# Channel blocks opened during the first batch's tail, V placed by GpSimd, pair 12 prepared a pair sooner, weights issued later

## Chip, cores and metric

One core of a Trainium2 chip. The metric is the device time of the kernel in microseconds (us), launch to end; the span in a profile is some 1.8 us shorter. Runs of one kernel scatter by up to 4 us here, mostly for a reason that the experiments show, so medians are given with the runs' granted TensorE clocks (1.0 is full rate, and the mean over a run is given). All runs with a recorded state are in the fast state. In the lines of the profile PE is TensorE, DVE VectorE, ACT ScalarE, POOL GpSimd and SPq SyncE, which issues DMAs; L with a number is a line of the kernel.

## The reference

Cosine attention for 8 batches, 12 heads, 448 positions, 64 channels a head, then a low-rank mixer and a channel network on the 768 channels:

```python
q_n = q / (norm(q) + 1e-06); k_n = k / (norm(k) + 1e-06)
attn = softmax(q_n @ k_n.T / tau)
x = attn @ v                                  # laid out as [batch, 448, 768]
h = x.transpose(0, 2, 1) @ U @ V              # rank 32
u = x + h.transpose(0, 2, 1)
out = u + relu(u @ w_ch1) @ w_ch2             # 768 -> 3072 -> 768
```

## The kernel before

The 48 pairs of heads (8 batches of 6) are numbered 0 to 47 and handled in groups, mostly of two pairs. A group's q, k and v are loaded by SyncE's queue, squared (ScalarE or GpSimd), reduced (VectorE), rooted (ScalarE), inverted, and q and k scaled. The scaled blocks are transposed by TensorE, from pair 12 on by the DMA. The first batch runs by a hand-written list of words; from pair 6 on, each pair's attention is interleaved with "fill" steps, the channel network of the batch before: 24 blocks of six matmuls with w1 (m1), then 24 steps of six matmuls with w2 (m2). The first batch's 48 steps are spread over pairs 6 to 12.

```python
# the tail of the first batch's list: w7 is seven filler matmuls, A, XT, H the mixer's steps,
# Ac and U its evictions, w1_i the issue of a quarter of w1 (GpSimd's DMA queue)
... V50 Ac4.v XT4 X50 V51 sq4k H4 X51
w7 U4.a A5 red4q Ac5.a XT5 H5 U5.a red4k w1_2 root4 w1_3 inv4 sc6q.v sc6k.v
# (cut)
load_w2(0, 0, 12); load_w2(0, 12, 24)
preps[4].values()
fill.extend(steps_m1(0) + steps_m2(0))
f(5)                       # five blocks ahead of pair 6's transposes
T(NP)
# (cut) preparation of pair 12's group: when its squares, reductions, root, scalings run
elif m == 2 * NP:
    at = [(m - 2, 0), (m - 2, 0), (m - 2, 6), (m - 2, 4), (m - 2, 3), (m - 2, 5)]
    when = [(m - 1, 0)] * 4
# (cut) loads: of pair m's group, by SyncE; the program order is the queue's order
put(m - 6, 4, lambda gi=gi: load(gi, "q", nc.sync))
put(m - 5, 5, lambda gi=gi: load(gi, "k", nc.sync))
put(m - 4, 3, lambda gi=gi: load(gi, "v", nc.sync))
```

Of the kernel before, what the change touches and what calls it, by code (L numbers as in the profile page):

```python
# [22 lines left out]
def kernel(  # L23
# [17 lines left out]
    nc = tc.nc  # L41
# [106 lines left out]
    def place_v(copy, rows):  # L148
        lo = V_raw[rows, 0:256].rearrange("r (p c) -> r c p", c=4)
        hi = V_raw[rows, 256:448].rearrange("r (p c) -> r c p", c=3)  # L150
        body = V_sb[rows, 0:384].rearrange("r (c p) -> r c p", p=128)
        copy(out=body[:, :, 0:64], in_=lo[:, 0:3, :])
        copy(out=body[:, :, 64:128], in_=hi)
        copy(out=V_sb[rows, 384:448], in_=lo[:, 3, :])

    def place_mixer():
        nc.scalar.copy(out=U_sb[:, :, 0:R], in_=U_raw)
        place_v(nc.scalar.copy, slice(0, R))

    def load_copies():  # L160

# [10 lines left out]
    def load_w2(half, n0, n1):  # L172
        cols = slice(half * HC, (half + 1) * HC)
        nc.gpsimd.dma_start(
            out=w2_sb[:, n0:n1, cols],
            in_=moe_w_ch2[n0 * 128:n1 * 128, cols].rearrange("(n p) d -> p n d", p=128))
# [407 lines left out]
    def f(n):  # L584
        for _ in range(n):
            fill.pop(0)()
# [18 lines left out]
    def T(n):  # L605
        step_T(*pairs[n])
# [10 lines left out]
    def Hs(n):  # L617
# [3 lines left out]



    ORDER = """
        sq0k.a red0k sq0q.a red0q root0 inv0 sc0q.v sc0k.v l3q l3k l2v w62 T0 sq1q.a sq1k.p w11
        Te0 red1q S00 sq2k.p S01 ex00 red1k w8 root1 S02 w26 sq2q.a inv1 red2k sc1k.p ex01 sc1q.p
        red2q ex02 S03 w6 ex03 val0 l3v T1 root2 val1 l4q l4k l4v V00 Te1 place inv2 S10 V01
        sc2q.v S11 ex10 w9 sc2k.v ex11 X01 sc3k.p S12 T2 X00 ex12 S13 sc3q.p Te2 A0 w3 sq3q.a
        Ac0.v S20 T3 sq3k.a w19 red3q ex13 red3k ex20 S21 V10 ex21 w1_0 V11 X10 S22 Te3 root3 val2
        l5q l5k l5v S23 ex22 inv3 XT0 H0 X11 sc4q.p ex23 S30 U0.v ex30 V20 sc4k.v S31 A1 ex31 S32  # L630
        X20 sc5q.p T4 Ac1.v ex32 Te4 V21 sc5k.p S33 X21 XT1 ex33 S40 val3 H1 ex40 A2 U1.v S41 V30
        Ac2.v ex41 S42 X30 T5 ex42 V31 Te5 S43 X31 ex43 S50 XT2 ex50 A3 S51 Ac3.v H2 V40 ex51 U2.v
        S52 X40 V41 w1_1 ex52 S53 X41 XT3 sq4q ex53 H3 A4 U3.a V50 Ac4.v XT4 X50 V51 sq4k H4 X51
        w7 U4.a A5 red4q Ac5.a XT5 H5 U5.a red4k w1_2 root4 w1_3 inv4 sc6q.v sc6k.v
    """
    bank1 = psum.tile([128, 512], FP, name="mp", tag="ps_m", bufs=2)
    spare = psum.tile([128, 512], FP, name="mp", tag="ps_m", bufs=2)
    copies = {"a": nc.scalar.copy, "v": nc.vector.tensor_copy}
    QK = {"q": 0, "k": 1}

    def word(w):
        w, _, eng = w.partition(".")
        if w.startswith("w1_"):
            i = int(w[3:])
            load_w1(768 * i, 768 * (i + 1))
        elif w[0] == "w":
            for _ in range(int(w[1:])):
                nc.tensor.matmul(out=spare[:, 0:128], lhsT=ident, rhs=ident, start=True, stop=True)
        elif w[0] == "l":
            load(int(w[1]), w[2], nc.sync)  # L650
        elif w == "place":
            place_mixer()
        elif w.startswith("sq"):
            preps[int(w[2])].square(QK[w[3]], eng == "a")
        elif w.startswith("red"):
            preps[int(w[3])].reduce(QK[w[4]])
        elif w.startswith("root"):
            preps[int(w[4])].root()
        elif w.startswith("inv"):
            preps[int(w[3])].invert()  # L660
        elif w.startswith("val"):
            preps[int(w[3])].values()
        elif w.startswith("sc"):
            gi, j = group_of[pairs[int(w[2])]]
            preps[gi].scale(QK[w[3]], j, {"v": V_, "p": P_}[eng])
        elif w.startswith("Te"):
            evict_T(*pairs[int(w[2])])
        elif w.startswith("ex"):
            exp_S(*pairs[int(w[2])], int(w[3]))
        elif w.startswith("XT"):  # L670
            pe_XT(*pairs[int(w[2])])
        elif w.startswith("Ac"):
            evict_A(*pairs[int(w[2])], copies[eng])
        else:
            at = pairs[int(w[1])]
            if w[0] == "T":
                pe_T(*at)
            elif w[0] == "S":
                pe_S(*at, int(w[2]))
            elif w[0] == "V":  # L680
                half = int(w[2])
                pe_V(*at, half, bank1 if half else
                     psum.tile([128, 512], FP, name="av", tag="ps_av", bufs=1))
            elif w[0] == "X":
                divide_V(*at, int(w[2]))
            elif w[0] == "A":
                pe_A(*at)
            elif w[0] == "H":
                pe_H(*at)
            else:  # L690
                assert w[0] == "U", w
                evict_H(*at, copies[eng])

    for w in ORDER.split():
        word(w)
    load_w2(0, 0, 12)
    load_w2(0, 12, 24)
    preps[4].values()
    fill.extend(steps_m1(0) + steps_m2(0))
    f(5)  # L700
    T(NP)
    preps[4].scale(0, 1, V_)
    preps[4].scale(1, 1, V_)
# [8 lines left out]
    for gi in range(5, len(groups)):  # L712
        m, g = first_pair[gi], preps[gi]
        scales = [(1, 0, P_), (1, 1, P_), (0, 0, V_), (0, 1, V_)]
        if m == NP + 2:
            at = [(NP, 0), (NP, 1), (NP + 1, 6), (NP, 5), (NP + 1, 0), (NP + 1, 1)]
            when = [(NP + 1, 2), (NP + 1, 5), (NP + 1, 2), (NP + 1, 5)]
            scales = [(1, 0, V_), (1, 1, V_), (0, 0, V_), (0, 1, V_)]
        elif m == NP + 4:
            at = [(NP + 2, 0), (NP + 2, 1), (NP + 2, 6), (NP + 2, 3), (NP + 2, 5), (NP + 2, 6)]  # L720
            when = [(NP + 3, 0), (NP + 3, 0), (NP + 3, 1), (NP + 3, 3)]
        elif m == 2 * NP:
            at = [(m - 2, 0), (m - 2, 0), (m - 2, 6), (m - 2, 4), (m - 2, 3), (m - 2, 5)]
            when = [(m - 1, 0)] * 4
            scales = [(1, 0, P_), (0, 0, P_), (1, 1, P_), (0, 1, P_)]
        else:
            d = 1 if m == 2 * NP + 2 else 0
            at = [(m - 3, 0), (m - 3, 0), (m - 3, 5)] + [(m - 2, i + d) for i in (1, 0, 2)]
            when = [(m - 2, i + d) for i in (3, 3, 4, 5)]

        put(*at[1], lambda g=g: g.square(1))
        put(*at[0], lambda g=g: g.square(0))
        put(*at[2], lambda g=g: g.values())
        put(*at[4], lambda g=g: g.reduce(1))
        put(*at[3], lambda g=g: g.reduce(0))
        put(*at[5], lambda g=g: g.root())
        put(*when[0], lambda g=g: g.invert())
        for x, w in zip(scales, when):
            put(*w, lambda g=g, x=x: g.scale(*x))
        if gi > 5 and m - 6 <= NP:  # L740
            put(*((NP, 3), (NP + 3, 0))[gi - 6], lambda gi=gi: load_all(gi))
        elif gi > 5:
            put(m - 6, 4, lambda gi=gi: load(gi, "q", nc.sync))
            put(m - 5, 5, lambda gi=gi: load(gi, "k", nc.sync))
            put(m - 4, 3, lambda gi=gi: load(gi, "v", nc.sync))
        if by_dma(m):
            put(m - 1, -1 if m > 2 * NP else 2, lambda m=m: T(m))
            put(m - 1, 0 if m > 2 * NP else 4, lambda m=m: T(m + 1))

    put(NP, 2, lambda: (load_w2(1, 0, 12), load_w2(1, 12, 24)))  # L750
    put(NP + 3, 0, load_copies)
    put(NP + 5, 6, place_copies)

# [16 lines left out]
    for n in range(NP, NPAIR + 1):  # L770
# [7 lines left out]
        if not late:  # L778
            if n % 2 == 0:

                order = [
                    (1, lambda: Sc(n, 0, 1)),
                    (0, done and (lambda: V(n - 1, 0))),
                    (1, None if by_dma(n + 1) else (lambda: T(n + 1))),
                    (0, lambda: Sc(n, 3)),
                    (1, done and (lambda: V(n - 1, 1))),
                    (0, done and (lambda: A(n - 1))),
                    (1, lambda: (Sc(n, 2), Sc(n + 1, 0))),
                    (1, done and (lambda: Hs(n - 1))),
                ]  # L790
            else:
                order = [
                    (1, lambda: Sc(n, 1, 2)),
                    (1, lambda: V(n - 1, 0)),
                    (0, lambda: Sc(n, 3)),
                    (1, lambda: V(n - 1, 1)),
                    (1, not by_dma(n + 1) and (lambda: T(n + 1))),
                    (1, lambda: A(n - 1)),
                    (0, lambda: Hs(n - 1)),
                ]  # L800
            last = p == 0 and done
            nf = len(fill) if last else 5
            spread(n, order, nf)
            if last:
                f(len(fill))
                fill.extend(steps_m1(b - 1) + steps_m2(b - 1))
            continue
# [80 lines left out]
```

## Time and profile before

| | kernel before |
|---|---|
| median of the 4 runs beside the changed kernel | 588.94 us (587.92 to 589.08) |
| TensorE busy | 571.9 of 585.8 us |
| wait of PE at pair 12 (for the DMA transposes) | 2.40 us, then 3.4 us at half clock |
| transposes of pair 12: issued, landed | 93.91 us, 100.23 us |
| w2's last part landed | 97.6 us |

Landings are read from the DMA records of the trace. The lines that carry the argument stand in the prediction. What to look for in them: PE is full from 105 us to the end, so everything that the change can win lies before, and there the DMA share is about 1.

### The profile page before, as it was taken

To read this page: it belongs to the slowest core of one execution; us is meant where nothing else is said; L and a number is where in the kernel's file an instruction comes from. 1 tells how busy PE (TensorE), PEld (TensorE's weight loads), DVE (VectorE), ACT (ScalarE), POOL (GpSimd) and SP (SyncE) were. 2 spreads that over 40 slices of the span, in tenths; PEclk is the share of its full clock that TensorE was granted. 3 is DMA by queue.
4 is the path that set the end of the run, shared out by engine and by line. 5 is a ranking of instruction groups with operands and counts; after the bars stand their busy time and mean duration, and the time that the engine had idled before them with its cause. 6 is when DMAs were issued, how large, how long until landed. Compare 5 with 4: busy or idle time off the path is not lost.

```text
span 585.8 us, 12308 instructions
## 1 busy us (share of the span) xinstructions
PE 571.9 (98%) x5087; PEld 329.4 (56%) x5087; DVE 260.9 (45%) x503; ACT 260.8 (45%) x449; POOL 187.7 (32%) x162
## 2 busy tenths in 40 slices
PE   7999998999999999999999999999999999999997
PEld 6664564655555555554565555655556555655564
DVE  7875762525345355544454265543455342220011
ACT  5965544265334555346423465345442474214200
POOL 8674356504145055234053142252250410000000
PEclk9999999999999999999999999999999999999999
DMA  6999999455375684684464754873645631222012
GB/s 166 203 235 234 236 239 230 115 118 120 79 160 129 123 144 113 133 172 94 107 148 120 163 110 99 159 159 84 139 119 122 135 64 25 59 62 44 8 47 55
DMA packets 138584, 74.25 MB, mean 127 GB/s; under 512 B 85568, under 2 KB 138352, under 8 KB 138528
## 3 DMA queue, kind: packets, MB, share of 16 engines
q1 hardware_dynamic: 128256, 62.77, 48.2%
q0 software_dynamic: 9728, 10.18, 10.2%
q8 instruction: 40, 0.66, 0.5%
q10 hardware_dynamic: 544, 0.51, 0.3%
q14 instruction: 16, 0.13, 0.1%
HBM read 52.19 MB, written 11.01 MB: 108 GB/s over the span
## 4 chain that ended last, share of the span: by engine, by line
PE 88%; DMA 5%; DVE 2%; issue 1%; ACT 1%; SPq 1%; POOL 1%; POOLq 0%; DVEq 0%
PE mp L538 36%; PE mp L511 35%; PE sc L329 5%; PE av L381 3%; PE up L381 2%; DMA qst<-in_q_dram 2%; DVE qk L269 1%; DMA vst<-in_v_dram 1%; DMA qkT<-qk 1%; PE av L374 1%; PE av L341 1%; PE tp L298 1%; PE up L374 1%; PE up L467 1%; ACT E L354 1%
## 5 line engine op out<-in xcount | busy, mean ns | idle before, releaser
L538 PE MATMUL mp<-w_sb,relu 128*128 128x384 bf16 x1344 | 234.8, 328 | 0.0
L538 PEld LDWEIGHTS <-relu 128*128 128x128 bf16 x1344 | 125.9, 98 | 90.5 <-issue 14.5
L511 PEld LDWEIGHTS <-w_sb 128*128 128x128 bf16 x1152 | 107.4, 98 | 101.4 <-issue 10.1
L515 ACT ACTIVATE relu<-mp 128x448 bf16<-128x448 f32 x164 | 89.1, 543 | 131.2 <-PE mp L511 131.2
L354 ACT ACTIVATE E<-sc 128x896 bf16<-128x896 f32 x144 | 125.0, 923 | 23.6 <-PE sc L329 22.7
L269 POOL TENSOR_TENSOR qk<-kst,inv 128x512 bf16<-128x512 f32 x41 | 49.5, 1226 | 257.9 <-DVE inv L263 257.9
L511 PE MATMUL mp<-uE,w_sb 128*128 128x448 bf16 x576 | 117.5, 353 | 0.0
L511 PE MATMUL mp<-uO,w_sb 128*128 128x448 bf16 x576 | 114.2, 353 | 0.0
L556 DVE TENSOR_TENSOR o_sb<-mp,ut 128x384 f32<-128x384 f32 x50 | 27.9, 557 | 131.2 <-PE mp L538 131.2
L249 DVE TENSOR_REDUCE ss<-sq 128x16 f32<-128x1024 f32 (+1 forms) x50 | 57.8, 1165 | 0.8 <-ACT sq L241 0.8
L517 DVE TENSOR_SCALAR relu<-mp 128x448 bf16<-128x448 f32 x28 | 17.4, 623 | 78.0 <-PE mp L511 77.7
L244 POOL TENSOR_TENSOR sq<-kst 128x1024 f32<-128x1024 f32 (+1 forms) x23 | 44.8, 1951 | 9.4 <-DMA kst<-in_k_dram 7.4
L269 DVE TENSOR_TENSOR qk<-qst,inv 128x512 bf16<-128x512 f32 x42 | 46.7, 1117 | 0.6
L329 PE MATMUL sc<-qkT 64*64 64x448 bf16 x576 | 42.6, 360 | 3.6 <-DMA qkT<-qk 2.4
L244 POOL TENSOR_TENSOR sq<-qst 128x1024 f32<-128x1024 f32 x21 | 43.2, 2058 | 7.4 <-DVE qkT L303 4.5
L381 PEld LDWEIGHTS <-E 128*128 128x128 bf16 x1152 | 45.0, 97 | 0.0
L277 POOL CAST v<-vst 128x1024 bf16<-128x1024 f32 (+1 forms) x25 | 26.9, 1080 | 14.9 <-DMA vst<-in_v_dram 11.0
L351 ACT ACTIVATE E<-av 128x448 bf16<-128x448 f32 x17 | 9.2, 541 | 47.3 <-PE up L341 47.3
L381 PE MATMUL av<-v,E 128*128 128x65 bf16 x648 | 29.1, 193 | 0.0
L392 DVE RECIPROCAL rd<-av 128x4 f32<-128x4 f32 x54 | 9.7, 179 | 39.0 <-PE av L381 39.0
L374 PEld LDWEIGHTS <-E 128*128 128x128 bf16 x192 | 18.1, 98 | 14.6 <-issue 0.8
L471 ACT CAST A_sb<-up 128x128 bf16<-128x128 f32 x18 | 4.7, 263 | 45.9 <-PE up L467 45.9
(99 smaller groups left out, 352.0 us busy)
## 6 DMA issues: line engine op xcount, KB each, us to landing
out_dram<-o_sb SPq DMA_DIRECT2D x109, 96.0 KB, 2.3
w_sb<-in_moe_w_ch_dram POOLq DMA_DIRECT2D x8, 1152.0 KB, 25.3
qst<-in_q_dram SPq DMA_DIRECT2D x23, 256.0 KB, 4.0
vst<-in_v_dram SPq DMA_DIRECT2D x46, 128.0 KB, 2.9
kst<-in_k_dram SPq DMA_DIRECT2D x44, 128.0 KB, 2.8
qst<-in_q_dram SPq DMA_DIRECT2D x23, 192.0 KB, 4.1
vst<-in_v_dram SPq DMA_DIRECT2D x46, 96.0 KB, 2.7
kst<-in_k_dram SPq DMA_DIRECT2D x44, 96.0 KB, 2.7
```

What stands on the lines that cost most here:

```text
L244: nc.gpsimd.tensor_mul(sq[:, 0:self.nh * 4, :], self.flat(t), self.flat(t))
L249: nc.vector.reduce_sum(self.ss[:, j, 0:self.nh * 4], self.sq[j][:, 0:self.nh * 4, :], axis=AX.X)
L269: eng.tensor_mul(qks[self.gi % 2][:, j, i, :, :, :], t[:, 2 * j:2 * j + 2, :, :].rearrange("p h c d -> p c h d"), iv.unsqueeze(3).to_broad ...
L277: nc.gpsimd.tensor_copy(out=self.flat(v65[self.s])[:, :, 0:D], in_=self.flat(vst[self.s]))
L329: nc.tensor.matmul(out=sc[o:o + 64, h, 0:S], lhsT=t[r, 1, c * 128 + o:c * 128 + o + 64], rhs=t[r, 0, 0:S], start=True, stop=True)
L354: nc.scalar.activation(out=e[:, 2 * c:2 * c + 2, 0:S], in_=sc[:, :, 0:S], func=AF.Exp)
L374: nc.tensor.matmul(out=av[:, i, :, :], lhsT=last_of(b, p)[:, ic * 128:(ic + 1) * 128], rhs=vv[:, 2 * j:2 * j + 2, 3, :], start=(i == 0), s ...
L381: nc.tensor.matmul(out=av[:, i, h, :], lhsT=e[:, 2 * c + h, ic * 128:(ic + 1) * 128], rhs=vv[:, 2 * j + h, c, :], start=False, stop=(i == ...
L511: nc.tensor.matmul(out=mp, lhsT=w1_sb[:, cc, f * 128:(f + 1) * 128], rhs=u[:, cc, 0:S], start=(cc == 0), stop=(cc == CC - 1))
L515: nc.scalar.activation(out=relu[:, f, o:o + S], in_=mp, func=AF.Relu)
L538: nc.tensor.matmul(out=mp, lhsT=relu[:, f, r0:r0 + 128], rhs=w2_sb[:, f, half * HC:(half + 1) * HC], start=(f == 0), stop=(b > 0 and f == ...
L556: nc.vector.tensor_add(o.rearrange("p (k d) -> p k d", d=128), mp.rearrange("p (k d) -> p k d", d=128), ut_of[(b, half)][:, :, c, :])
```

## The change

Its intent: fill the idle moments of TensorE at the end of the first batch with four channel blocks, held open in the score banks until the last two channel chunks arrive; take V's placement off ScalarE; prepare pair 12's group sooner so that PE does not wait for its transposes; and send w1's last parts and w2 later, so that q, k and v come sooner.

```diff
-    def place_mixer():
+    def place_u():
         nc.scalar.copy(out=U_sb[:, :, 0:R], in_=U_raw)
-        place_v(nc.scalar.copy, slice(0, R))
-        ... Te1 place inv2 ... sq3q.a
+        ... Te1 plU inv2 ... sq3q.a plV.p         # V by GpSimd, ahead of w1_0
-        ... V51 sq4k H4 X51
-        w7 U4.a A5 red4q Ac5.a XT5 H5 U5.a red4k w1_2 root4 w1_3 inv4 sc6q.v sc6k.v
+        ... V51 sq4k H4 U4.a X51
+        M004 A5 red4q Ac5.a XT5 M104 H5 U5.a M045 M145 M205 red4k M056 M156 R0 R1 M256 root4 M306
+        inv4 sc6q.v sc6k.v R2 R3
+    def pe_m1(fb, lo, hi): ...   # block fb, channel chunks lo to hi, in a score bank; R: its relu
-    load_w2(0, 0, 12); load_w2(0, 12, 24)
     preps[4].values()
-    fill.extend(steps_m1(0) + steps_m2(0)); f(5)
+    load_w1(1536, 2304)
+    fill.extend(steps_m1(0)[4:] + steps_m2(0)); f(2)
         elif m == 2 * NP:
-            at = [(m - 2, 0), (m - 2, 0), (m - 2, 6), (m - 2, 4), (m - 2, 3), (m - 2, 5)]
-            when = [(m - 1, 0)] * 4
+            at = [(m - 3, 6), (m - 2, 0), (m - 1, 0), (m - 2, 2), (m - 2, 5), (m - 2, 6)]
+            when = [(m - 2, 7)] * 4
-            put(m - 1, -1 if m > 2 * NP else 2, lambda m=m: T(m))
+            put(m - 1, -1 if m > 2 * NP else 0, lambda m=m: T(m))       # and T(m + 1): 4 -> 1
-    put(NP, 2, lambda: (load_w2(1, 0, 12), load_w2(1, 12, 24)))
+    put(NP, 2, lambda: load_w1(2304, 3072))
+    put(NP, 3, lambda: (load_w2(0, 0, 12), load_w2(0, 12, 24)))
+    put(NP + 1, 2, lambda: (load_w2(1, 0, 12), load_w2(1, 12, 24)))
-                    (1, done and (lambda: V(n - 1, 1))),
+                    (1, (lambda: V(n - 1, 1)) if done else None),        # pair 6: fill over 5 places
```

The list's lines are cut at the dots and some comments are mine; the squares of pair 8's group also change their places by one.

> **What bounds the kernel now.** I read the page first, then the table of windows, PE's waits, PE's timeline where it was not full, the chain of waits, and the DMA records.
>
> The page gives TensorE 571.9 us of 585.8. The windows (us, length, then busy time of PE, PEld, DVE, ACT, POOL, granted clock, DMA share, GB/s) say where the rest is:
>
> ```profile
> 15.00:30.00 15.00, 13.76 (x214) 9.30 (x212) 13.15 (x29) 13.96 (x24) 9.29 (x9) 1.00 0.98 214
> 45.00:60.00 15.00, 13.63 (x120) 7.00 (x119) 9.89 (x14) 9.10 (x16) 7.25 (x5) 1.00 1.16 234
> 75.00:90.00 15.00, 15.00 (x167) 9.76 (x165) 8.90 (x18) 7.46 (x14) 7.37 (x8) 1.00 1.25 235
> 90.00:105.00 15.00, 12.60 (x119) 7.42 (x118) 2.73 (x8) 4.89 (x8) 9.85 (x10) 0.89 1.02 217
> 105.00:120.00 15.00, 15.00 (x125) 8.97 (x122) 9.22 (x14) 5.45 (x10) 7.74 (x5) 1.00 0.39 102
> ```
>
> After 105 us PE is full until the last output, so only what happens before can be won. Two things stand out: the clock falls to 0.89 in 90 to 105 us, and until then the DMA share is about 1, after it 0.39. PE's own timeline:
>
> ```profile
> 37.52 0.55 PE L648 MATMUL mp<-ident 128*128 128x128 bf16 x7
> 38.22 0.38 PE L414 MATMUL mp<-X,U_sb 128*128 128x128 bf16 x4 [0.15 <-DVE X L393]
> 38.96 0.36 PE L439 MATMUL up<-V_sb,A_sb 128*128 128x448 bf16 x1 [0.15 <-ACT A_sb L420]
> 49.22 0.62 PE L298 MATMUL tp<-ident,qk 128*128 128x128 bf16 x8 [0.80 <-DVE qk L269]
> 53.17 0.38 PE L329 MATMUL sc<-qkT 64*64 64x448 bf16 x4 [0.56 <-ACT E L351]
> 100.28 0.65 PE L329 MATMUL sc<-qkT 64*64 64x448 bf16 x8 [2.40 <-DMA qkT<-qk]
> 100.86 3.68 PE L538 MATMUL mp<-w_sb,relu 128*128 128x384 bf16 x12
> 104.88 2.11 PE L538 MATMUL mp<-w_sb,relu 128*128 128x384 bf16 x12
> ```
>
> The largest single wait is 2.40 us for pair 12's transposes. The twelve matmuls behind it take 3.68 us, the same twelve later 2.11 us: another 1.6 us. The event costs 4.0 us. The chain of waits in front of it:
>
> ```profile
> 66.73 10.79 DMA qst<-in_q_dram
> 77.54 7.43 DMA vst<-in_v_dram
> 91.53 2.38 POOL qk L269 x3
> 93.91 6.32 DMA qkT<-qk
> ```
>
> The transpose takes 6.32 us here, but 3.25 us at 118.95 us, when the weights have come. In the DMA records its packets begin only near 97 us, behind pair 16's q (landed 98.7) and an output (99.35). So preparation is one half of this wait and a full DMA queue the other.
>
> [...] its clock record shows half rate for 3.413 us from 100.65 us. The gap was 2.40 us[...].
> [...] while w2 streams, its queue writes about 117 KB per us and the SyncE queue 119; alone, the weights write 200, SyncE's queue 270.
> [...] the scaling on VectorE takes 0.69 us, and in one case 1.7 us more because it overlapped a GpSimd square:
>
> ```profile
> 46.78 2.38 DVE L269 TENSOR_TENSOR qk<-kst,inv 128x512 bf16<-128x512 f32 x1
> 46.31 2.30 POOL L244 TENSOR_TENSOR sq<-qst 128x1024 f32<-128x1024 f32 x1 [4.46 <-DVE qkT L303]
> ```
>
> **The change part by part.** The order of instructions per engine shows the same PE work except seven filler matmuls fewer.
>
> Opened blocks. From 37.52 us to the first channel block at 39.16 us, PE needs 0.22 + 0.20 + 0.19 = 0.61 us for the last A, XT and H steps; the other 1.03 us are filler and waits. Four blocks of six matmuls at 0.19 us go in between. My count of the new order (24 opened plus 12 more matmuls before pair 6's transposes, 6.9 us, plus 0.61) puts those transposes at 45.0 us, as before (44.92), with one block more behind them: **1.0 us gained** in work done. The price: the root of group 4 now stands behind two relus on ScalarE, at about 42.3 instead of 40.45 us; with the old 3.16 us from root to scaled k this is 45.4 us, so up to 0.5 us can be lost again, or 1.5 us if a GpSimd square falls on it.
>
> Spread of pair 6. Five fill steps are spread over five places instead of three, so a block stands ahead of the score matmul that waited 0.56 us: **0.5 us gained**. The 0.80 us at 49.22 us is probably changed or moved with its GpSimd square.
>
> V on GpSimd. ScalarE loses three copies (0.54 + 0.45 + 0.30, about 1.2 us with overlap). But at 15 to 22 us the chain runs over VectorE (scaling, X, eviction), and PE runs 31 fillers there. I give it 0.2 us. GpSimd issues w1's first part 1.2 us later; it landed at 30.8 us and is first read at 37.5 us: no cost.
>
> Pair 12's group. Squares and reductions come sooner, but the inverse stays behind the same H eviction (89.33 us) on VectorE, and the root moves behind two exps of 0.9 us. Root at 89.7, inverse 90.7, two GpSimd scalings of 1.05 us: 92.9 us against an issue at 93.91 us. The transposes are thus **1.0 us sooner** against the work around them, not a pair sooner, plus whatever PE has won.
>
> w1 and w2 later. Part 2 leaves after group 4's values (42 us), part 3 and w2 after group 5's squares. Group 5's q and k, which landed up to 51.8 us, should land some 6 us sooner. But the bytes stay: what is saved early is asked back later. I counted both queues forward with the rates above. For the kernel before this gives w2's last part at 97.4 us (landed 97.6) and the transpose at 99.5 us (landed 100.2). For the changed kernel: w2's second part 78 to 80 us, needed about 79.5; the last part 98 to 100 us, needed after pair 12's first scores; the transpose at 98.5 to 99.7 us, whatever I assume for the start. With the count's error of 0.7 us: **99.6 us**.
>
> Sum. PE will be ready for pair 12 near 97 us and still wait some 2.5 us, until 99.6 instead of 100.28 us (0.7 us), with one channel step (1.1 us) done more, and the half clock again. Together 1.8 us. [...] 589.1 - 1.8 - 0.7 = **586.6 us**.
>
> **The rivals.** (1) The wait at pair 12 vanishes: 1.0 + 0.5 + 4.0 = 5.5 us, 583.5 us. For it: the transposes are asked for 1 to 2 us sooner, and the second output chunk ahead of them is done a step sooner, so the queue may have run empty. Against it: nothing takes bytes away, and the weights stream until about 98 us instead of 97.
> (2) A wait for w2 takes its place: w2 is issued some 15 us later, its second and last parts come close to their need. If the last comes at 102 us, PE waits for it instead, with the half clock: 590 us. For it: 1 us of margin in my count. Against it: while SyncE's queue is empty (58 to 67 us in the count) the weights run at 200 and catch up.
> (3) Pair 6 waits for scalings held up by group 5's squares, now sooner on GpSimd: 1.5 us lost at 45 us, but then swallowed by the later wait for the DMA: 587.3 us.
>
> **Range and chances.** The middle is the DMA-bound case; 583 us is rival 1 with V's copies counted; 589.4 us is rival 2 in a mild form. Two per cent are 11.8 us, more than all idle time that PE has between 35 and 105 us, so faster by over 2% is almost excluded, and slower would need two new waits of w2 size. 0.01, 0.97, 0.02.
>
> **What would show it.** Opened blocks right: no filler and no gap over 0.1 us between 36 and 42 us, pair 6's transposes near 45 us. Spread right: no wait for an exp near 53 us. DMA-bound right: pair 12's scores start at 99 to 100 us after a wait of 2 to 3 us for the transpose, its issue near 92 us, and it takes over 6 us. Wrong: its start near 96 to 97 us without a wait (rival 1), a PE wait on w_sb near 79 or 99 us (rival 2), clock 1.00 in 90 to 105 us. The whole would be wrong if waits arose after 105 us, where I assume none.

Passages cut here and in the expectations told of the hardware what no run of this case shows. What is left beside the cuts is from the trace of the kernel before ("its clock record" is that trace's). The rates can be read there: in 58 to 64 us w2's queue moved 0.70 MB beside SyncE's 0.72 MB, in 87.3 to 89.3 us 0.39 MB almost alone, and SyncE's queue 0.54 MB alone in 31 to 33 us. The sum came to 589.1 - 1.8 - 0.7 = 586.6 us. The 1.8 us are the sooner landing (0.7) and the channel step (1.1); of the term of 0.7 us, a half clock of 1.6 us spared in 4 cases of 10, the sentence is cut: the share was my estimate, and no run stood behind it.

## The result

585.91 us in the median (585.5 to 586.6, 4 runs) against 588.94 us: ratio 0.9953, interval 0.9936 to 0.9971. Ratios in this document are the mean of one kernel's fast runs over that of the other's fast runs of the same rounds, so not quite the ratio of the medians. The class is "same" (within 2%); the prediction was 586.6 us.

The windows of the changed kernel (columns as in the prediction):

```profile
15.00:30.00 15.00, 13.31 (x208) 9.14 (x206) 13.11 (x29) 12.93 (x21) 10.48 (x12) 1.00 0.91 198
45.00:60.00 15.00, 13.42 (x108) 6.50 (x106) 10.04 (x12) 8.92 (x16) 11.49 (x9) 1.00 1.14 237
75.00:90.00 15.00, 14.16 (x163) 9.17 (x160) 10.14 (x18) 5.73 (x11) 7.37 (x7) 1.00 1.24 238
90.00:105.00 15.00, 12.97 (x134) 8.11 (x131) 3.03 (x9) 7.18 (x12) 10.85 (x11) 1.00 1.11 228
```

PE is idle longer than before in 75 to 90 us (0.84 us, before none), hardly less in 90 to 105 us (2.03 instead of 2.40 us), but the clock there is 1.00 instead of 0.89. PE's timeline (start, length, what ran, in brackets the idle time before it and what ended it), the lines that answer to those in the prediction:

```profile
38.01 0.92 PE L650 MATMUL sc<-uE,w_sb 128*128 128x448 bf16 x4
50.67 0.62 PE L297 MATMUL tp<-ident,qk 128*128 128x128 bf16 x8 [1.53 <-DVE qk L268]
82.19 0.36 PE L427 MATMUL up<-ident,X 128*128 128x128 bf16 x4 [0.84 <-DVE qkT L302]
101.93 0.57 PE L328 MATMUL sc<-qkT 64*64 64x448 bf16 x8 [2.03 <-DMA qkT<-qk]
102.43 2.12 PE L537 MATMUL mp<-w_sb,relu 128*128 128x384 bf16 x12
```

The fillers are gone, a block stands there; the wait for an exp at 53 us is gone. Two waits are new or longer: 1.53 us for pair 7's scaling (0.80 before) and 0.84 us ahead of an XT step. Pair 12's scores start at 101.93 us, later than before (100.28), but with one step more behind them, and the twelve matmuls after them run at full speed. The chain:

```profile
93.87 1.08 POOL qk L268 x2
94.95 6.94 DMA qkT<-qk
```

The transposes are issued 1 us later than before, not sooner, and take 0.6 us longer. What the two waits are is seen on VectorE and GpSimd (lines one and two: pair 7's k and the square across it; three and four: pair 11's q and the square across it):

```profile
48.23 2.38 DVE L268 TENSOR_TENSOR qk<-kst,inv 128x512 bf16<-128x512 f32 x1
47.80 2.26 POOL L243 TENSOR_TENSOR sq<-kst 128x1024 f32<-128x1024 f32 x1
79.33 2.21 DVE L268 TENSOR_TENSOR qk<-qst,inv 128x512 bf16<-128x512 f32 x1
79.10 1.89 POOL L243 TENSOR_TENSOR sq<-qst 128x1024 f32<-128x1024 f32 x1 [0.35 <-DMA qst<-in_q_dram]
```

The scaling, 0.69 us elsewhere, took 2.38 and 2.21 us here, where a square of GpSimd lay across it; in both pairs of lines it ended 0.55 us after the square did. The change brought both squares sooner, under scalings: pair 7's k scaling had lain under another square before (prediction), so that wait grew, and the one at 82 us is new.

My theory after this: PE is bound at pair 12 by SyncE's DMA queue, which the change does not relieve; the gain is a step of work done sooner, plus the half clock that a shorter wait spares. Rivals: the sooner preparation is what counts; the later weights are what counts; the clock only follows.

### The profile page after: what moved, and what is told of

Its sections match the earlier page's. It is cut to its first block, busy times and chain, and to the rows that moved or that the text cites. A ratio compares the mean times of both kernels' runs of the same rounds, so it can differ in the third digit from the quotient of the medians.

```text
span 584.8 us, 12295 instructions
## 1 busy us (share of the span) xinstructions
PE 570.1 (97%) x5080; PEld 328.5 (56%) x5080; DVE 262.2 (45%) x501; ACT 261.0 (45%) x448; POOL 189.1 (32%) x165
## 4 chain that ended last, share of the span: by engine, by line
PE 92%; DVE 3%; ACT 2%; DMA 2%; issue 1%; POOL 0%; ACTq 0%; POOLq 0%; DVEq 0%
PE mp L537 37%; PE mp L510 36%; PE sc L328 6%; PE av L380 3%; PE up L380 2%; DVE qk L268 2%; DMA qkT<-qk 1%; PE av L373 1%; ACT E L353 1%; PE tp L297 1%; PE av L340 1%; PE sc L650 1%; PE up L373 1%; PE up L466 1%; PE av L480 1%
## 5 line engine op out<-in xcount | busy, mean ns | idle before, releaser
L510 PEld LDWEIGHTS <-w_sb 128*128 128x128 bf16 x1128 | 105.2, 98 | 99.5 <-issue 10.0
L510 PE MATMUL mp<-uE,w_sb 128*128 128x448 bf16 x552 | 112.9, 353 | 0.0
L268 DVE TENSOR_TENSOR qk<-qst,inv 128x512 bf16<-128x512 f32 x42 | 50.5, 1209 | 0.7 <-DVE inv L262 0.2
L516 DVE TENSOR_SCALAR relu<-mp 128x448 bf16<-128x448 f32 x26 | 16.2, 623 | 76.3 <-PE mp L510 75.9
```

Source lines behind the costliest of these rows:

```text
L268: eng.tensor_mul(qks[self.gi % 2][:, j, i, :, :, :], t[:, 2 * j:2 * j + 2, :, :].rearrange("p h c d -> p c h d"), iv.unsqueeze(3).to_broad ...
L510: nc.tensor.matmul(out=mp, lhsT=w1_sb[:, cc, f * 128:(f + 1) * 128], rhs=u[:, cc, 0:S], start=(cc == 0), stop=(cc == CC - 1))
```

## Experiments

Twelve jobs (the changed kernel again, and eleven edited kernels) in three sessions; within a session on one chip, beside the same runs of the kernel before. All were correct. One run of each was profiled, so where in a kernel the half clock fell is known for that run alone; of the others only the mean clock is.

**The changed kernel again.**

> The changed kernel unchanged, on the chip of the three runs beside it, so that they can be compared with it in one place. 585.9 us, 0.5% under the kernel before. The profile of before had 3.4 us at half clock and the one of after none; if that is where half of the gain lies, the granted clock of the runs should be near 1.000 in all runs here and near 0.997 in most runs of before.

Measured: 585.96 us (585.56 to 588.31, 6 runs), ratio 0.9974 (0.9955 to 0.9993) to 588.29 us of before. Over the three sessions before ran 33 times; I sort the runs at a mean granted clock of 0.998, since one stretch of 3.41 us at half rate takes 3.41 / 2 / 586 = 0.003 off the mean:

| kernel | runs at 0.998 or more | their mean | runs below | their mean |
|---|---|---|---|---|
| before | 6 of 33 | 586.66 us | 27 | 588.37 us |
| changed (first and second job) | 8 of 10 | 585.90 us | 2 | 587.89 us |

At full clock the change is worth 0.76 us. The means of all runs (588.06 and 586.30 us) differ by 1.76 us; the other 1.0 us goes with the rarer half clock. (The sets are not of the same sessions: the table has no run of before from the first job, whose clocks are not on record.)

**Fillers in the wait of the kernel before.** Does the clock cause the time?

```diff
+                if n == FIRST2:        # pair 12: 30 matmuls on the identity ahead of its scores
+                    warm()
```

> The kernel before with 30 filler matmuls (128x128 on the identity, about 1.7 us in all) ahead of pair 12's first scores, inside the wait of 2.4 us for the transposes. They do no useful work. Clock theory: [...] every run shows a granted clock of 0.999 to 1.000, and the time falls from 588.3 to about 586.7 us, as the two runs of before that had clock 1.000. Rival (clock and time only go together because both follow a longer wait): time stays at 588 us.

Measured: 586.55 us (586.4 to 586.78, 6 runs, clocks 0.998 to 1.000), ratio 0.9975. The profile's timeline of PE:

```profile
97.33 1.84 PE L784 MATMUL mp<-ident 128*128 128x128 bf16 x30
100.76 0.57 PE L329 MATMUL sc<-qkT 64*64 64x448 bf16 x8 [1.60 <-DMA qkT<-qk]
101.27 2.12 PE L538 MATMUL mp<-w_sb,relu 128*128 128x384 bf16 x12
```

The scores start no sooner, yet 1.4 us are gone from the median, and the scatter of 4 us shrinks to 0.4. The half clock was the cause of most of the kernel's scatter, and thirty useless matmuls reach the ratio that the changed kernel had in the session before (0.9974).

**Loads behind the transposes**, in the changed kernel. Is it the queue?

```diff
-            put(m - 6, 4, lambda gi=gi: load(gi, "q", nc.sync))
+            put(*((m - 6, 4) if m != 2 * NP + 4 else (m - 5, 3)), lambda gi=gi: load(gi, "q", nc.sync))
-            put(m - 4, 3, lambda gi=gi: load(gi, "v", nc.sync))
+            put(*((m - 4, 3) if m != 2 * NP + 2 else (m - 3, 2)), lambda gi=gi: load(gi, "v", nc.sync))
```

> Only the order of SyncE's queue: pair 14's v (448 KB) and pair 16's q (448 KB) are issued behind pair 12's transposes instead of ahead of them. Queue theory (mine): the transposes no longer stand behind 896 KB that land at 93 to 101 us; issued near 94 us they land at 98 to 99.5 us, PE waits under 0.5 us at pair 12 and the end comes 1.7 to 2.5 us sooner (583.4 to 584.2 us). Preparation theory: issue and landing stay at 95 and 101.9 us and the time at 585.9 us.

Measured: 582.69 us (582.1 to 583.11, 4 runs, all at clock 1.0), ratio 0.9908 (0.989 to 0.9926). SyncE's queue and PE in the profile:

```profile
92.89 4.05 SPq L312 DMA_TRANSPOSE qkT<-qk  x2
97.00 0.67 SPq L211 DMA_DIRECT2D vst<-in_v_dram  x1
```

```profile
98.08 0.57 PE L328 MATMUL sc<-qkT 64*64 64x448 bf16 x8 [0.24 <-DMA qkT<-qk]
```

The loads stand behind now, the transposes land at 98.04 us, 5.15 us after their issue instead of 6.84 to 6.94, and the wait is 0.24 us. What lay ahead in the queue was the bound. (w2's last part landed at 95.90 us instead of 99.39 to 99.87, so the moved loads had also held up the weights; the runs do not tell their place in the queue from their bytes. The XT wait was absent in this profile too: the scaling of pair 11's q began at 78.27 us, 0.14 us ahead of GpSimd's square, and took 0.68 us; in the changed kernel's second profile it began 0.03 us behind the square and took 2.40. That is part of why the issue is sooner.)

**Loads behind, in the kernel before.**

> The kernel before with only the two loads (pair 14's v, pair 16's q) issued behind pair 12's transposes. Queue theory: the transposes, issued at 93 to 94 us, land near 98.5 us instead of 100.2, PE waits about 0.6 us instead of 2.4, no half clock: 588.3 - 1.8 - 1.6 = 585 us or less, that is at least as much as the whole change gave, without any part of it. Rival (the parts of the change are needed for it): 588 us.

The edit is the same. Measured: 584.84 us (583.44 to 588.43, 6 runs), ratio 0.9953, the same as the whole change had. Its three runs at clock 1.0 have 583.44 to 584.59 us, the others (0.994 to 0.997) 585.08 to 588.43 us. As no wait for the transposes is left in its profile, the half clock of these three probably came from elsewhere than pair 12. The profile shows another wait, which I had not counted:

```profile
27.31 0.28 PE L374 MATMUL av<-v,E 128*128 128x130 bf16 x2 [1.50 <-POOL v L277]
26.23 1.03 POOL L277 CAST v<-vst 128x1024 bf16<-128x1024 f32 x1 [5.52 <-DMA vst<-in_v_dram]
```

The first line is PE's, the second GpSimd's. Pair 2's values wait for the last of four v loads, issued by SyncE at 20.01 us, just after GpSimd issued w1's first part (19.81 us); it landed at 26.07 us. In the profile of before the two issues are at 19.45 and 19.46 us, the load first, and it landed at 23.19 us. So in these two profiles a race of a few tenths of a us decided whether PE waited there.

**V on ScalarE again.**

```diff
-  ... plU inv2 ...  sq3q.a plV.p
+  ... plU plV.a inv2 ...  sq3q.a
```

> Only V placed by ScalarE again, all else as changed. My step gave V on GpSimd 0.2 us, as VectorE and PE carry the chain at 15 to 22 us: same time within 0.4 us (585.6 to 586.4), start of the last stretch of the first batch (first score matmul of pair 2) unchanged. Rival (ScalarE is the bound there, 93% busy): 1.0 us longer.

Measured: 586.29 us (586.06 to 588.98, 6 runs), ratio 0.9979 (0.9955 to 1.0003): not to be told from 585.96. But the profile shows the lost race, with w1 issued at 19.62 us and the v load at 19.84 us, and the half clock after it (0.83 in 25 to 35 us):

```profile
27.80 0.28 PE L373 MATMUL av<-v,E 128*128 128x130 bf16 x2 [2.18 <-POOL v L276]
```

With V's three copies on GpSimd (0.52 + 0.43 + 0.28 us), w1's first part leaves at 20.6 to 21.1 us in the profiles of the changed kernel and its variants, behind that v load (19.5 to 20.1 us), which then landed by 22.3 to 23.4 us. That is what the part does: it delays the weights past a load. How many runs lose the race without it is not known, but five of these six runs are below a clock of 0.998, against 2 of 10 with V on GpSimd. In the profiled one the half clock (3.41 us from 29.41 us) lies behind this wait; it cost little at the end, since PE then waited 1.28 us for pair 12's transposes instead of 1.94 to 2.03.

**Pair 12's preparation taken back**, first in the changed kernel, then with the loads moved too.

```diff
-            at = [(m - 3, 6), (m - 2, 0), (m - 1, 0), (m - 2, 2), (m - 2, 5), (m - 2, 6)]
-            when = [(m - 2, 7)] * 4
+            at = [(m - 2, 0), (m - 2, 0), (m - 2, 6), (m - 2, 4), (m - 2, 3), (m - 2, 5)]
+            when = [(m - 1, 0)] * 4      # and T(m), T(m + 1) at 2 and 4 as before
```

> Only the preparation of pair 12's group as in the kernel before (squares, reductions, root, inverse, places of the transposes), all else as changed. My step: its advance of 1.0 us is eaten by the queue, so the landing stays within 0.5 us of 101.5 us and the time at 586 us; the wait of 1.0 us of the XT step near 81.5 us, which came with the sooner square on GpSimd, goes, so it may even be 585.5 us. Rival (the sooner preparation is what shortened the wait): landing 1 to 2 us later and 587.5 us.

Measured: 588.39 us (586.0 to 590.02, 6 runs), ratio 1.0003. I had expected 586 us; the rival's figure came out, but not by its mechanism:

```profile
101.34 0.57 PE L328 MATMUL sc<-qkT 64*64 64x448 bf16 x8 [3.50 <-DMA qkT<-qk]
```

```profile
92.57 7.04 SPq L312 DMA_TRANSPOSE qkT<-qk  x2
```

The transposes were issued at 92.57 us, sooner than with the part (94.31 and 94.95 us), and landed at 101.30 us, against 101.16 and 101.88 us in the two profiles of the changed kernel. So the part made the issue later, not sooner, and the queue hid it. PE, without the XT wait, arrived 1.4 to 2.1 us sooner and waited 3.50 us in one piece, and five of six runs fell to a clock of 0.992 to 0.997. The one that did not, which is the profiled one, took 586.0 us, as the changed kernel. So by my reading the part "gains" 2.4 us in the median (over two sessions) by splitting a wait in two; that the half clock of the five fell at this wait was not seen.

> Loads behind the transposes, and pair 12's preparation as in the kernel before. Taken back without the loads moved it left the landing at 101.3 us and cost 2.4 us in the median [...]. With the queue out of the way [...] the transposes are issued near 92.5 to 93.5 us and land at 98 us, PE waits under 0.5 us, and the time is within 0.5 us of 582.7 us. If the sooner preparation is worth something by itself, it is over 583.5 us.

Measured: 583.0 us (582.09 to 585.66, 6 runs, clocks 0.998 to 1.000), ratio 0.9923: with the queue cleared, the preparation is worth nothing that shows (582.69 with it). The profiled run, the slowest, had the wait of my second rival:

```profile
83.53 1.14 PE L537 MATMUL mp<-w_sb,relu 128*128 128x384 bf16 x6 [1.86 <-DMA w_sb<-in_moe_w_ch_dram]
```

w2's second part landed at 83.49 us there, the whole stream of weights being late there: w1's third part was issued at 45.22 us, against 40.4 to 43.0 us in the other profiles with late weights.

**Opened blocks taken back**, in the changed kernel and with the loads moved.

```diff
-        ... H4 U4.a X51 M004 A5 ... M306 inv4 sc6q.v sc6k.v R2 R3      f(2)
+        ... H4 X51 w7 U4.a A5 red4q Ac5.a XT5 H5 U5.a red4k root4 inv4 sc6q.v sc6k.v      f(5)
```

> The four opened blocks taken back (filler, plain order of the tail, five blocks ahead of pair 6's transposes), all else as changed. My sum gave the opened blocks 1.0 us of work done sooner at 45 us. If pair 12 is bound by the DMA queue, that ms step reaches the end only through work done while PE waits there: the wait at pair 12 then shrinks from 2.0 to about 1 us and the end is about 1.0 us later than the changed kernel (587 us), since the landing of the transpose is fixed. Rival (preparation bound): the landing moves with PE, the wait stays 2.0 us, the end is 1.0 us later as well. The time alone does not tell them apart, the length of the wait does.

Measured: 586.43 us (585.3 to 587.76, 6 runs), ratio 0.9975 (0.9955 to 0.9994), not to be told from 585.96. The wait at pair 12 was 1.71 us instead of 1.94, the transposes landed at 100.31 instead of 101.16 us: the landing moved with PE, so the queue's end is not a fixed point, as I had put it.

> Loads behind the transposes, and the opened blocks taken back. With the queue out of the way PE's own order counts, so the 1.0 us that my step gave the opened blocks must show now: 583.5 to 583.9 us against 582.7. If the time stays at 582.7 us, the blocks gained nothing (root behind two relus, wait for the scaling longer).

Measured: 583.91 us (583.52 to 584.52, 6 runs), ratio 0.9929, against 582.69 us and 0.9908 with the blocks (another session, before at 588.14 and 588.29 us; the intervals 0.9914 to 0.9945 and 0.989 to 0.9926 overlap). The difference, 1.2 us, is what was expected of the blocks, 1.0 us.

**Weights early again**, in the changed kernel.

```diff
+    load_w1(1536, 2304); load_w1(2304, 3072); load_w2(0, 0, 12); load_w2(0, 12, 24)
     preps[4].values()
-    load_w1(1536, 2304)          # and the later issues go; w2's second half at (NP, 2) as before
```

> w1's last parts and w2 issued as early as in the kernel before, all else as changed. If moving them later helped: pair 12's transposes land later than 101.9 us and the end is up to 1 us later. If my count is right that the bytes are only put off: w2's last part lands near 97.6 instead of 99.9 us, the transposes near 100.5 us instead of 101.9, group 5's k near 52 instead of 47.6 us, and the time is the same or up to 1 us less (585 to 586 us).

Measured: 587.38 us (585.17 to 589.2, 6 runs), ratio 0.9987 (0.9966 to 1.0008), not to be told from the kernel before. w2's last part landed at 99.10 us and the transposes at 100.45 us (100.5 expected). Its one run at full clock, 585.17 us, is under the changed kernel's full-clock mean of 585.90; the other five runs are at clocks of 0.994 to 0.997. In the profile, which is of the run at full clock, the wait at pair 12 is 2.56 us in one piece; that it is what brings the half clock to the five is likely, not seen.

**Group 5's q squared on ScalarE**, loads behind; then with the weights early too.

```diff
-        put(*at[0], lambda g=g: g.square(0))
+        put(*at[0], lambda g=g, m=m: g.square(0, m == NP + 2))
```

> The changed kernel with the two loads behind pair 12's transposes (as in the run that took 582.7 us), and group 5's square of q on ScalarE instead of GpSimd. There PE waited 1.1 us at 49.6 us for a scaling on VectorE that lay under GpSimd's squares. If that contention is its cause, the k scaling takes 0.7 instead of 2.4 us, the wait falls under 0.3 us, and, as nothing else holds PE back before pair 12 now, the time falls by 0.8 to 1.1 us to about 581.8 us. Rival: the square of k, which stays on GpSimd, moves under the scaling instead: no change.

Measured: 584.08 us (582.43 to 586.79, 6 runs), ratio 0.9935. The rival held: the square of k moved under the scaling (47.11 and 47.18 us), which took 2.38 us again, PE waited 0.80 us. Three of the runs are at 585 us and more at full clock; the profiled one is not among them, so their cause stays open. A late w2, as in the line above at 83.53 us, is a candidate that I have not shown for them.

> As the run with group 5's q on ScalarE, and w1's last parts and w2 issued early as in the kernel before. If the later weights are worth nothing once the queue is in the right order: within 0.5 us of that run (581.8 us). If the later weights help by loading group 5 sooner: 1 us longer; if they cost, because w2 streams until 99 us: up to 0.5 us shorter.

Measured: **581.86 us** (581.24 to 582.37, 5 runs, all at clock 1.0), ratio 0.9894 (0.9879 to 0.991), the fastest of the study. Windows and PE's largest wait from 45 us on:

```profile
45.00:60.00 15.00, 14.84 (x130) 7.77 (x128) 9.87 (x16) 10.59 (x18) 5.41 (x4) 1.00 1.16 234
90.00:105.00 15.00, 15.00 (x157) 9.59 (x155) 6.28 (x16) 6.69 (x12) 11.04 (x12) 1.00 1.01 213
```

```profile
79.89 0.36 PE L427 MATMUL up<-ident,X 128*128 128x128 bf16 x4 [0.56 <-DVE qkT L302]
```

With the weights early, group 5's k comes only at 52 us, so its square (52.41 us) is clear of the scalings by itself, and PE is full in 90 to 105 us. The later weights of the change are not needed once the queue is in order: the interval lies wholly under that of the run with later weights (0.9911 to 0.996). Whether they cost 2.2 us in the median or only in some runs is open, as the cause of that kernel's three long runs is.

## Why the prediction was right, and where it was not

**Opened blocks, 1.0 us.** Right: no filler and one gap over 0.1 us (0.16 at 36.41 us) in 36 to 42 us, pair 6's transposes at 45.65 us where 45.0 was said; taken back without the queue in the way, 1.2 us. The profiles show it too: from pair 12's first score to the end the kernels with the blocks need 482.88 to 482.91 us, those without, at full clock, 483.87 to 483.88 us (fillers, loads behind in the kernel before, blocks taken back twice). So what the change has at full clock is this 1.0 us, less a later start of those scores: 101.93 and 101.20 us, against 100.76 us in the profile with fillers.

**Spread of pair 6, 0.5 us.** The wait for an exp is gone, as said; its worth was not measured alone.

**Pair 6 or 7 and GpSimd's squares (third rival).** It came, at pair 7: 1.53 and 1.28 us in the two profiles instead of 0.80. That it is "swallowed" by the later wait was too simple: when PE's position moved (blocks taken back), the landing moved with it, by 0.85 us.

**V on GpSimd, 0.2 us, "no cost".** The time does not contradict it, but the step looked at the wrong thing: in the profiles it is the delay of w1's first part that matters, and it is a benefit.

**Pair 12's group, 1.0 us sooner.** Failed, in its sign: the issue was at 94.95 and 94.31 us, not near 92, and with the part taken back at 92.57 us. PE's own position was later by the two waits of 1.3 to 1.5 and 0.8 to 1.0 us, of which I had counted the first as optional and the second, which the sooner square brought, not at all. That the queue eats such a difference was right: landed at 101.30 us without the part, 101.16 and 101.88 with it.

**Landing of the transposes, 99.6 us.** The mis-sized term: 101.16 to 101.88 us. The mechanism (bytes ahead in the queue, weights until 99.4 to 99.9 us where 98 to 100 was counted) is shown by moving two loads, 3.3 us in the median. The start of the count was too early: pair 14's q, issued at 64.77 us in the kernel before, was issued at 66.36 us, and the count had taken it sooner, not later.

**Half clock spared in 4 cases of 10.** The share was my estimate, not shown by a run (its sentence is cut from the prediction). It was spared in 8 of 10, and before in only 6 of 33, though the wait shrank only from 2.40 to about 2.0 us. Which part did that is open: taking back the preparation, the later weights or V's place each left one run of six at full clock, taking back the blocks four. This error (0.6 to 0.7 us to the good) and the landing's (1.6 to 2.3 us to the bad), together with the higher median of before that the sum started from (589.1 against 588.3 and less in the later sessions), made 586.6 come so near to 585.9. These errors cancel, and that is luck. At full clock the sum reads 1.8 us, and 0.76 us was measured.

**After 105 us** no wait arose, as assumed.

## What to carry to other kernels

When a transfer that PE waits for stands behind prefetches in the same queue, look first at what lies ahead of it there: moving two loads that nobody needed yet behind it gave as much as the whole change, and 3.3 us more on top of it. Count a wait on TensorE for itself and for a chance of half clock after it: in the profiles here gaps of 2.18 and 2.40 us had 3.41 us of it behind them, at a cost of up to 1.7 us, gaps of 1.94, 2.03, 2.56 and 3.50 us had none, so the length alone does not decide. If the wait cannot be removed, matmuls on a constant inside it may be worth having: thirty of them took 1.4 us off the median here. And where an engine's work is moved sooner, see what it will lie across: here two squares moved under scalings and gave 1.5 us of new waits.
